# A transformer block on one core: the first folded weight is stored and loaded at earlier steps, and half of the sums of the second MLP weight stand beside the first MLP product

## The chip, the core and the metric

The kernel runs on one core of one Trainium2 chip. The core has TensorE (PE; its weight loads are PEld), VectorE (DVE), ScalarE (ACT), GpSimd (POOL) and SyncE (SP), which here only issues transfers. Each engine works through its own list of instructions in the order in which they were written, and waits at an instruction until what it needs is there. The metric is the device time of one execution in microseconds (us).

## The reference

The block computes two pre-norm sublayers in fp32 on x of 2048 x 1024:

```python
h = x + _A_ref(_layernorm(x), A_wqkv, A_w_phi, A_wo)
h2 = h + _B_ref(_layernorm(h), B_w1, B_w2)
# _A_ref: q, k, v = split(x @ wqkv), 32 heads of 32
#   pq, pk = q @ w_phi, k @ w_phi (by head)
#   phi = concat(softmax(p), softmax(-p))         # 64 features by head
#   o = phi_q (phi_k^T v) / (phi_q sum(phi_k) + 1e-6);  return o @ wo
# _B_ref: relu(x @ w1) @ w2, with w1 1024 x 3584 and w2 3584 x 1024
```

## The kernel before, in words

**Products.** Every large product is made with three matmuls of 128 x 512 (lines 181 to 183, `mm3`): each operand is cut into a high and a low half, and high x high, high x low and low x high are added up in PSUM. A weight tile of 128 x 512 that is cut so is called a unit. ACT makes the high half (L124), and POOL or DVE the low half, weight minus high half (L128). `Units` loads raw tiles into a ring of 6 and cut units into a ring of 10; a unit's place comes free when its last product is done. In an MLP stage one unit serves four products.

**Order.** All work is a list of items for TensorE: first 32 items for k and v of the first eight row tiles (four slabs of 256 columns, `kv`, eight tiles each), 16 for q (two slabs), then the same 48 for the other eight row tiles (the second half), 32 for the output projection, and then the two MLP products. In the list each item of these first stages has eight steps, a step being the three matmuls of one unit; an MLP item has four. The program counts steps from 0; step 64 opens the second kv slab, 256 the first q slab, 384, 448, 512 and 576 the kv slabs of the second half, 640 its first q slab. Everything else is hung on a step with `when(step, function)`: it is written into its engine's list behind that step's matmuls. The steps are set by hand, and they say the place in each engine's list, not a time.

**Fold.** w_phi is multiplied into the q and k weights on the chip, two blocks of 128 rows at a time (`fold_part`, p = 0 to 7). TensorE multiplies, DVE turns the result (L309, `fold_turn`) into `wp`, `fold_store` stores it to DRAM in two halves of 512 KB (wpk, L317), and `fold_ready` allows the units of that slab to be loaded (L330 and L331). The fold p = 1 belongs to the second kv slab.

**Sums of the MLP weights.** The two MLP products are made by a scheme of Strassen's kind with seven products in place of eight; it needs sums of the blocks of w1 and w2. 56 sets make them: `t_load` loads 512 KB (tile b, L357), `t_sum` makes four subtractions of 128 x 256 on POOL (L367), `t_store` stores 512 KB (t, L370). The first 28 sets belong to w1, the others to w2, whose sums are first read in the second MLP product.

**Beside the slabs.** For each kv item DVE makes the two softmaxes (tiles kmx, ke, ksm, kphi) and POOL adds phi_k up (zacc, L457). At the end of a slab of the second half DVE combines the kv state (kd, L480), which TensorE transposes (L487), and TensorE sums zacc over the rows (`z_sum`, L495). Six early units of the attention (u = 0 to 5) multiply exp(q) by that sum on POOL while later slabs run (`early_load`, `early_sums` L560, `early_reduce`, `at_den`, `early_scale` L570). `ln_power` (L229 to L231) makes 1/sqrt(var + eps) on POOL for row tiles whose statistics are taken ahead.

Of the kernel before, what the change touches and what calls it, by code (L numbers as in the profile page):

```python
# [9 lines left out]
F32 = mybir.dt.float32  # L10
# [5 lines left out]
P = 128  # L16
S = 2048
D = 1024
# [3 lines left out]
NT = S // P  # L22
HT = NT // 2
NK = D // P
NC = DFF // P
NP = NC // 2
# [113 lines left out]
def kernel(  # L140
# [17 lines left out]
    lnp = ctx.enter_context(tc.tile_pool(name="lnp", bufs=2))  # L158
# [29 lines left out]
    def do(n, k, f, *args):  # L188
        at[n, k].append((f, args))
# [17 lines left out]
    xin, xst, xnt = {}, {}, {}  # L207
# [52 lines left out]
    tsp = kps.enter_context(tc.tile_pool(name="tsum", bufs=1, side="right"))  # L260
    folds = ExitStack()
    fp = folds.enter_context(tc.tile_pool(name="fold", bufs=2))
# [89 lines left out]

    def t_load(w, p, j, place):
        cols = slice(256 * j, 256 * (j + 1))
        b = place.tile([P, 4, 256], F32, name="b", bufs=2)
        src = (w1 if w == 1 else w2)[2 * p:2 * p + 2, :, :, cols]
        sp.dma_start(b, src.rearrange("a b p f -> p (a b) f"))  # L357
        for r in range(2):
            for c in range(2):
                tsum[j, r, c] = b[:, 2 * c + r if w == 1 else 2 * r + c, :]  # L360
        tsum[j] = b
# [483 lines left out]
    def item(gen, *args, keys):  # L845
        items.append((gen, args + (keys,)))
        steps.extend((k,) for k in keys)
        return len(items) - 1

    kv_n, q_n, wo_n, up_n, down_n = {}, {}, {}, {}, {}  # L850
# [9 lines left out]
    for b, tiles in enumerate(groups):  # L860
        for hf in range(2):

            pairs = b == 0 and hf == 0
            for j in range(0, 4, 2 if pairs else 1):
# [3 lines left out]
                for half in range(2):  # L868
                    n = item(wo_pair, tiles[j:j + 2], hf, half, keys=[("wo", hf, 4 * half + k // 2) for k in range(8)])
# [18 lines left out]
    def x_part(t):  # L888
        return [x[t * P:(t + 1) * P, :]]
# [6 lines left out]
    def when(step, f, *args):  # L896

        if step < 8 * first_up:
            do(step // 8, step % 8, f, *args)
        else:  # L900
            do(first_up + (step - 8 * first_up) // 4, step % 4, f, *args)
# [4 lines left out]
    for t in range(1, NT):  # L906
        n = t - 1 if t < HT else q_n[1, t - HT] + 1
        turn = 8 * n + 1
        if t < HT:
            stages = X_STEPS.get(t, (turn - 22, turn - 12, turn - 9, turn - 6, turn, turn + 3))  # L910
        else:

            early = 80 + 16 * (t - HT)
            when(early, ln_load, ("s", t), x_part(t))
            when(early + 14, ln_stats, ("s", t))
            when(early + 14, xin.pop, ("s", t))
            when(early + 17, ln_power, ("s", t))
            load_ = turn - 88 + 8 * (t - HT) if t < HT + 4 else turn - 36
            stages = (load_, None, None, turn - 8, turn, turn + 3)
        for step, f, *args in zip(stages, (ln_load, ln_stats, ln_power, ln_norm), [("x", t)] * 4):  # L920
            if step is not None:
                when(step, f, *args, *([x_part(t)] if f is ln_load else []))
        do(n, 0, x_open, t)
        for j in range(2):
            when(stages[4 + j], ln_turn, ("x", t), j, lambda t=t: xT[t])
# [7 lines left out]
    for p, n in zip(range(1, 8), (3, 8, 12, 16, 20, 24, 28)):  # L933
        do(n, 6 if p > 1 else 7, fold_part, p)
        if p > 1:
            when(8 * n + 10, fold_turn, p, (0, 1))
        for j in range(2):
            when(8 * n + 6 + 14 + 2 * j, fold_store, p, j)
            when(8 * n + 6 + 24 + 2 * j, fold_ready, p, j)
        do(max(n - 2, 1), 0, wt_load, p, sp)  # L940


# [73 lines left out]
    for u in range(32):  # L1016
        start = 8 * (a0 + u) if u >= 8 else 8 * (last_kv + 4) + 19 * u // 2
        slack = 6 if u < 5 else 0
        for step, f in ((-8 if u < 12 else -1, at_load), (6, at_sums), (10, at_reduce), (13, at_den), (16, at_inverse), (19, at_scale),
                        (25, at_turn), (30 + slack, at_num), (32 + slack, at_low)):  # L1020
            if u >= EARLY or f in (at_load, at_scale, at_turn, at_num, at_low):
                when(max(start + step, 8 * (last_kv + 4)), f, u)
        if u < EARLY:
            start = 8 * (kv_n[1, u // 2, NT - 1] + 4 + 4 * (u % 2))
            for step, f in ((0, early_load), (9, early_sums), (14, early_reduce), (16, at_den), (18, at_inverse),
                            (20, early_scale)):
                when(start + step, f, u)
# [12 lines left out]
    up0 = 8 * first_up  # L1040
# [9 lines left out]
    def up_step(b, p, m):  # L1050

        return up0 + 4 * (up_n[b, p, m] + 1 - first_up)

    for j, m in enumerate(UP):

        for g in range(2):
            step = up0 + (8 * j + (-62, -32)[g] if j < 4 else 6 * (j - 4) + 10 + 2 * g)
# [4 lines left out]
            step = up_step(0, NP - 1, m) + 3 * j  # L1062
# [10 lines left out]

    for n, (w, p, j) in enumerate((w, p, j) for w in (1, 2) for p in range(NP) for j in range(2)):
        step = 24 + 10 * n
        if step > 8 * q_n[1, 0] - 20:
            step += 64
        far = step + 20 < 8 * q_n[0, 0]  # L1080
        when(step, t_load, w, p, j, fp if far and n % 4 > 1 else tsp)
        for k in range(4):
            when(step + (12 if far else 7) + k, t_sum, j, k)
        when(step + (19 if far else 13), t_store, w, p, j)

    for b in range(2):
        for m in DOWN:
            n = down_n[b, m, NP - 1] + 1
            name, more = {1: "x1", 5: "x4", 6: "x2", 4: "x3"}.get(m), \
# [123 lines left out]
```

## Time and profile before

| what | value |
|---|---|
| median of 3 runs | 1909.78 us (1909.72 to 1910.68) |
| the profiled execution's own time | 1910.06 us |
| its span | 1908.3 us |
| busy share PE, DVE, ACT, POOL | 99%, 55%, 39%, 51% |
| HBM traffic over the span | 225 GB/s |

A row of a timeline gives the start in us from the span's start, the duration in us, the engine, the line, the operation, the tiles (out<-in) and, in brackets, how long the engine stood idle before it and what ended that. "SPq" is the issue of a transfer by SP, not the transfer itself. A row of the waits view gives the total in us, the number of times and the longest. A row of windows gives the stretch in us, its length, then the busy us (and instructions) of PE, PEld, DVE, ACT and POOL, the granted TensorE clock, the mean share of the 16 DMA engines and GB/s.

### The profile page before, as it was taken

Reading aid. Unit: us, or ns where it says so; the run is one execution under the profiler, and the core shown is the slowest. Engines: PE = TensorE matmul, PEld = TensorE weight load, DVE = VectorE, ACT = ScalarE, POOL = GpSimd, SP = SyncE. Lnnn points to the kernel's source line nnn. Section 1 sums busy time; section 2 is a strip of 40 time slices with the busy share of each in tenths; the row PEclk is TensorE's granted clock in tenths of the full one; section 3 lists DMA queues with packets and bytes.
Section 4 is the critical chain, followed back from the end, with each engine's and each line's share of the span. In section 5 each row is a group of like instructions: output and inputs, shape, how many; then the busy total and the mean of one; then the engine's idle time right before and its main releaser. Section 6 shows DMA issues by size and latency. Waiting matters only on the chain.

```text
span 1908.3 us, 31967 instructions
## 1 busy us (share of the span) xinstructions
PE 1889.7 (99%) x11640; PEld 1539.3 (81%) x11640; DVE 1048.7 (55%) x1752; ACT 741.6 (39%) x1318; POOL 969.1 (51%) x935
## 2 busy tenths in 40 slices
PE   8999999999999999999999999999999999999999
PEld 7677788877777777888888888888888888888887
DVE  6788678767679766445544564344433333343333
ACT  4322235222223222245455564444444444444442
POOL 3688842789945988323333222222244444444443
PEclk9999999999999999999999999999999999999999
DMA  6699885656565667696776897566677677777775
GB/s 195 204 322 318 270 266 195 205 194 210 190 217 174 203 222 235 212 292 218 259 252 229 276 289 224 176 193 194 213 239 228 192 238 234 241 213 220 216 215 177
DMA packets 292733, 432.17 MB, mean 226 GB/s; under 512 B 24160, under 2 KB 150368, under 8 KB 292576
## 3 DMA queue, kind: packets, MB, share of 16 engines
q1 hardware_dynamic: 275680, 413.36, 68.8%
q10 hardware_dynamic: 16896, 16.78, 2.6%
q8 instruction: 91, 1.49, 0.3%
q14 instruction: 66, 0.54, 0.1%
HBM read 292.68 MB, written 137.36 MB: 225 GB/s over the span
## 4 chain that ended last, share of the span: by engine, by line
PE 86%; POOL 6%; DMA 4%; issue 1%; DVE 1%; ACT 1%; SPq 0%; POOLq 0%; DVEq 0%; ACTq 0%
PE mm L181 22%; PE mm L182 21%; PE mm L183 21%; PE ac L181 4%; PE ac L182 4%; PE ac L183 4%; POOL b L367 3%; PE tp L182 2%; PE tp L181 2%; PE tp L183 2%; POOL w L128 2%; DMA b<-in_w_dram 2%; PE tp L631 1%; DMA t<-b 1%; PE tp L244 1%
## 5 line engine op out<-in xcount | busy, mean ns | idle before, releaser
L128 POOL TENSOR_TENSOR w<-raw,w 128x512 fp32r<-128x512 f32 x355 | 473.6, 1336 | 730.0 <-ACT w L124 686.1
L124 ACT ACTIVATE w<-raw 128x512 fp32r<-128x512 f32 x686 | 409.4, 626 | 522.4 <-PE mm L183 249.9
L128 DVE TENSOR_TENSOR w<-raw,w 128x512 fp32r<-128x512 f32 x331 | 271.3, 820 | 533.5 <-ACT w L124 533.2
L182 PE MATMUL mm<-w,xT 128*128 128x512 f32 x768 | 302.6, 394 | 7.1 <-POOL w L128 6.8
L181 PE MATMUL mm<-w,xT 128*128 128x512 f32 x768 | 309.4, 403 | 0.0
L183 PE MATMUL mm<-w,xT 128*128 128x512 f32 x768 | 301.1, 392 | 0.0
L181 PE MATMUL mm<-hT,w 128*128 128x512 f32 x672 | 262.9, 391 | 0.0
L183 PE MATMUL mm<-hT,w 128*128 128x512 f32 x672 | 261.9, 390 | 0.0
L182 PE MATMUL mm<-hT,w 128*128 128x512 f32 x672 | 261.8, 390 | 0.0
L367 POOL TENSOR_TENSOR b<-b 128x256 f32<-128x256 f32 x224 | 184.2, 822 | 73.0 <-DMA b<-in_w_dram 63.2
L182 PEld LDWEIGHTS mm<-w,xT 128*128 128x128 f32 x768 | 145.1, 189 | 40.4 <-POOL w L128 10.7
L181 PEld LDWEIGHTS mm<-w,xT 128*128 128x128 f32 x768 | 145.1, 189 | 34.5 <-issue 3.8
L183 PEld LDWEIGHTS mm<-w,xT 128*128 128x128 f32 x768 | 145.1, 189 | 30.9 <-DVE xT L178 0.4
L181 PE MATMUL mm<-w 128*128 128x512 f32 x392 | 152.7, 390 | 0.0
L182 PE MATMUL mm<-w 128*128 128x512 f32 x392 | 152.7, 389 | 0.0
L183 PE MATMUL mm<-w 128*128 128x512 f32 x392 | 152.7, 389 | 0.0
L183 PEld LDWEIGHTS mm<-hT,w 128*128 128x128 f32 x672 | 126.2, 188 | 26.4
L181 PEld LDWEIGHTS mm<-hT,w 128*128 128x128 f32 x672 | 126.3, 188 | 25.7
L182 PEld LDWEIGHTS mm<-hT,w 128*128 128x128 f32 x672 | 126.3, 188 | 25.6
L181 PEld LDWEIGHTS mm<-w 128*128 128x128 f32 x392 | 73.6, 188 | 15.2
L183 PEld LDWEIGHTS mm<-w 128*128 128x128 f32 x392 | 73.6, 188 | 15.2
L182 PEld LDWEIGHTS mm<-w 128*128 128x128 f32 x392 | 73.6, 188 | 15.2
(165 smaller groups left out, 3111.1 us busy)
## 6 DMA issues: line engine op xcount, KB each, us to landing
raw<-t SPq DMA_DIRECT2D x224, 256.0 KB, 4.0
raw<-ad SPq DMA_DIRECT2D x196, 256.0 KB, 3.0
raw<-in_w_dram SPq DMA_DIRECT2D x168, 256.0 KB, 3.1
b<-in_w_dram SPq DMA_DIRECT2D x56, 512.0 KB, 4.9
t<-b SPq DMA_DIRECT2D x56, 512.0 KB, 4.6
ad<-c SPq DMA_DIRECT2D x112, 256.0 KB, 3.6
ad<-s SPq DMA_DIRECT2D x84, 256.0 KB, 3.9
ed<-qe ACTq DMA_DIRECT2D x32, 512.0 KB, 4.3
```

Of the source, the lines that this page charges most:

```text
L124: nc.scalar.activation(w[:, 0, :], raw[1], AF.Copy)
L128: eng.tensor_tensor(out=w[:, 1, :], in0=raw[1], in1=w[:, 0, :].bitcast(F32), op=ALU.subtract)
L181: pe.matmul(ps, a_hi, b_hi, start=first, stop=False, skip_group_check=more)
L182: pe.matmul(ps, a_hi, b_lo, start=False, stop=False, skip_group_check=more)
L183: pe.matmul(ps, a_lo, b_hi, start=False, stop=last, skip_group_check=more)
L244: pe.transpose(pt[:, k, :], xn[:, (4 * j + k) * P:(4 * j + k + 1) * P], ident)
L367: pool.tensor_tensor(out=tsum[j, *out], in0=tsum[j, *a], in1=tsum[j, *b], op=ALU.subtract)
L631: pe.matmul(banks[g][32 * c:32 * (c + 1), 0:P], kvL[rows, 4 * q + 2 * sd + h // 4, 32 * (h % 4):32 * (h % 4 + 1)], phT[rows, :, c, sd, :], ...
```

## The change

It has four parts. The store of the fold p = 1 and the release of its units are hung on earlier steps: store at 39 and 41 (before 44 and 46), release at 46 and 48 (before 54 and 56). The sets of sums get a table of steps: the first 22 stay, four stand at 264 to 294 (before, six at 244 to 294), two at 364 and 374; 14 stand at steps 10, 24 and 38 of each kv slab of the second half, with one more at step 2 of the second and third (before, 28 sets ten steps apart from 368 to 638); the last 14, all of w2, are hung on steps of the first MLP product of the second row half, 25 apart, and use the buffers `xin` of the layer norms. The early units start 4 steps (even u) or 18 steps (odd u) earlier. `ln_power` of the statistics taken ahead stands two steps later.

```diff
     def t_load(w, p, j, place):
         cols = slice(256 * j, 256 * (j + 1))
-        b = place.tile([P, 4, 256], F32, name="b", bufs=2)
+        if place is lnp:
+            b = lnp.tile([P, D], F32, name="xin").rearrange("p (a f) -> p a f", a=4)
+        else:
+            b = place.tile([P, 4, 256], F32, name="b", bufs=2)
...
-            when(early + 17, ln_power, ("s", t))
+            when(early + 19, ln_power, ("s", t))
...
         for j in range(2):
-            when(8 * n + 6 + 14 + 2 * j, fold_store, p, j)
-            when(8 * n + 6 + 24 + 2 * j, fold_ready, p, j)
+            lag = 8 * n + 6 + 2 * j + (3 if p == 1 else 0)
+            when(lag + (6 if p == 1 else 14), fold_store, p, j)
+            when(lag + (13 if p == 1 else 24), fold_ready, p, j)
...
         if u < EARLY:
-            start = 8 * (kv_n[1, u // 2, NT - 1] + 4 + 4 * (u % 2))
+            start = 8 * (kv_n[1, u // 2, NT - 1] + 3) + 4 + 18 * (u % 2)
...
-    for n, (w, p, j) in enumerate((w, p, j) for w in (1, 2) for p in range(NP) for j in range(2)):
-        step = 24 + 10 * n
-        if step > 8 * q_n[1, 0] - 20:
-            step += 64
-        far = step + 20 < 8 * q_n[0, 0]
-        when(step, t_load, w, p, j, fp if far and n % 4 > 1 else tsp)
+    sets = [(w, p, j) for w in (1, 2) for p in range(NP) for j in range(2)]
+    places = [24 + 10 * n for n in range(22)] + [264, 274, 284, 294, 364, 374]
+    slabs = [8 * kv_n[1, q, HT] for q in range(4)]
+    places += sorted([slab + step for slab in slabs for step in (10, 24, 38)] + [slabs[1] + 2, slabs[2] + 2])
+    places += [up0 + 440 + 25 * n for n in range(14)]
+    for n, (step, (w, p, j)) in enumerate(zip(places, sets, strict=True)):
+        far = n < 22
+        when(step, t_load, w, p, j, lnp if step > up0 else fp if far and n % 4 > 1 else tsp)
         for k in range(4):
             when(step + (12 if far else 7) + k, t_sum, j, k)
         when(step + (19 if far else 13), t_store, w, p, j)
```

The changed kernel's lines are numbered 3 higher from `t_load` on: L360 is the load of a set, L370 its subtraction, L373 its store.

SP, in the first slab, before (t_0 is the stored sum of the first set, wpk_75 the folded weight of the second slab, raw its units):

```order
L214 DMA xin<-in_x_dram 128x1024
L357 DMA b<-in_w_dram 128x4x256
L370 DMA t_0_310<-b 512x1x256
L317 DMA wpk_75<-wp 128x4x256
L357 DMA b<-in_w_dram 128x4x256
L317 DMA wpk_75<-wp 128x4x256
L274 DMA wt<-in_wqkT_dram 128x1024 x2
L370 DMA t_0_310<-b 512x1x256
L357 DMA b<-in_w_dram 128x4x256
L330 DMA raw<-wpk_75 128x256
L331 DMA raw<-in_wv_dram 128x256
```

The same place now:

```order
L214 DMA xin<-in_x_dram 128x1024
L360 DMA b<-in_w_dram 128x4x256
L317 DMA wpk_75<-wp 128x4x256 x2
L373 DMA t_0_310<-b 512x1x256
L360 DMA b<-in_w_dram 128x4x256
L330 DMA raw<-wpk_75 128x256
L331 DMA raw<-in_wv_dram 128x256
```

Both stores of the folded weight moved ahead of the first sum's store, and the units' loads ahead of the two loads wt, of another sum's store and of one load of a set. POOL's and ACT's lists are the same there.

POOL, at the start of the second half's first q slab, before (w is a low half, b a sum, xl the product of an early unit, smq its scale):

```order
L367 TENSOR_TENSOR b<-b 128x256 x3
L128 TENSOR_TENSOR w<-raw,w 128x512 x2
L457 TENSOR_TENSOR zacc_359<-zacc_359,kphi 128x512
L128 TENSOR_TENSOR w<-raw,w 128x512
L367 TENSOR_TENSOR b<-b 128x256
L128 TENSOR_TENSOR w<-raw,w 128x512
L367 TENSOR_TENSOR b<-b 128x256
L128 TENSOR_TENSOR w<-raw,w 128x512
L367 TENSOR_TENSOR b<-b 128x256
L128 TENSOR_TENSOR w<-raw,w 128x512
L367 TENSOR_TENSOR b<-b 128x256
L560 TENSOR_TENSOR xl<-xl,zb 128x1024
```

Now:

```order
L563 TENSOR_TENSOR xl<-xl,zb 128x1024
L370 TENSOR_TENSOR b<-b 128x256 x2
L460 TENSOR_TENSOR zacc_359<-zacc_359,kphi 128x512
L594 TENSOR_TENSOR xtz<-xtz,smq 128x32
L598 TENSOR_TENSOR qden<-xtz 128x16
L128 TENSOR_TENSOR w<-raw,w 128x512 x2
L460 TENSOR_TENSOR zacc_359<-zacc_359,kphi 128x512
L573 TENSOR_TENSOR smq<-smq,qden 128x4x8
L128 TENSOR_TENSOR w<-raw,w 128x512 x4
```

The sums between the low halves are gone, and the early unit's product and its two small products stand ahead of them. Low halves that DVE makes are not in this list; in a q slab of the second half POOL makes all.

POOL, where the moved sums begin, beside the first MLP product (the sums are written to xin):

```order
L128 TENSOR_TENSOR w<-raw,w 128x512 x17
L370 TENSOR_TENSOR xin<-xin 128x256 x4
L128 TENSOR_TENSOR w<-raw,w 128x512 x3
L370 TENSOR_TENSOR xin<-xin 128x256 x4
L128 TENSOR_TENSOR w<-raw,w 128x512 x3
```

There was nothing but low halves here; now four sums follow every three low halves, or stand singly between them, 14 times.

## The prediction

> **What bounds the kernel now.** I read the page's busy times first, then the waits of TensorE, then its timeline at each wait, then the stretches by window.
>
> ```profile
> span 1908.3 us, 31967 instructions
> PE 1889.7 (99%) x11640; PEld 1539.3 (81%) x11640; DVE 1048.7 (55%) x1752; ACT 741.6 (39%) x1318; POOL 969.1 (51%) x935
> PE mm L182 <- POOL w L128: 6.8, 6, 3.1
> PE tp L487 <- DVE kd L480: 1.4, 1, 1.4
> ```
>
> TensorE is busy 99% of the span. An edit that moves work between POOL, DVE and SP and leaves the matmuls as they are can win only what TensorE waits, and what it loses at a lower clock after a wait. The waits view names two causes within reach: a low half that POOL makes (L128), and the combined kv state of a slab that DVE makes late (L480). The timeline shows where:
>
> ```profile
> 72.53 0.50 PE L182 MATMUL mm<-w,xT 128*128 128x512 f32 x1 [0.34 <-POOL w L128]
> 74.91 0.50 PE L182 MATMUL mm<-w,xT 128*128 128x512 f32 x1 [0.73 <-POOL w L128]
> 79.65 0.80 PE L182 MATMUL mm<-w,xT 128*128 128x512 f32 x1 [3.08 <-POOL w L128]
> ...
> 422.03 0.50 PE L182 MATMUL mm<-w,xT 128*128 128x512 f32 x1 [0.50 <-POOL w L128]
> ...
> 435.15 0.92 PE L487 MATMUL tp<-ident,kd 128*128 128x128 f32 x4 [1.36 <-DVE kd L480]
> ...
> 522.29 0.50 PE L182 MATMUL mm<-w,xT 128*128 128x512 f32 x1 [1.40 <-POOL w L128]
> ```
>
> The same view of waits, for the stretch from 200 to 260 us, gives one more (at 232 us, the first q slab); the windows give the clock behind two of them, and the pace of an undisturbed stretch:
>
> ```profile
> PE mm L182 <- POOL w L128: 0.7, 1, 0.7
> ...
> 79.30:82.70 3.40, 3.05 (x7) 2.05 (x8) 3.31 (x6) 0.00 (x0) 3.40 (x4) 0.50 0.22 74
> 523.00:526.40 3.40, 3.40 (x10) 2.67 (x9) 1.12 (x1) 0.00 (x0) 3.40 (x2) 0.51 0.87 250
> 1137.00:1375.00 238.00, 238.00 (x1052) 197.19 (x1051) 101.45 (x139) 104.96 (x179) 58.18 (x44) 1.00 0.64 197
> ```
>
> The granted clock is 0.50 and 0.51 for 3.40 us behind the waits at 79 and 522 us, which costs 3.40 x 0.50 = 1.70 and 3.40 x 0.49 = 1.67 us. So the change can reach: A, second kv slab, 0.34 + 0.73 + 3.08 + 1.70 = 5.85; B, first q slab, 0.7; C, 422 us, 0.5; D, 435 us, 1.36; E, first q slab of the second half, 1.40 + 1.67 = 3.07. Together 11.5 us. From 1137 to 1375 us TensorE starts 1052 matmuls in 238 us, 0.226 us each: a step of three is 0.68 us.
>
> [...]
>
> **The first fold (term A).** SP held the store of the folded weight back:
>
> ```profile
> 46.23 1.40 DVE L309 STREAM_TRANSPOSE wp<-tp 128x256 f32<-128x256 f32 x4
> ...
> 55.34 0.60 SPq L370 DMA_DIRECT2D t<-b  x1
> 55.99 0.62 SPq L317 DMA_DIRECT2D wpk<-wp  x1
> 56.65 1.04 SPq L357 DMA_DIRECT2D b<-in_w_dram  x1
> 57.74 1.32 SPq L317 DMA_DIRECT2D wpk<-wp  x1
> 62.90 0.59 SPq L330 DMA_DIRECT2D raw<-wpk  x1
> ...
> 63.53 0.58 ACT L177 ACTIVATE xT<-tp 128x512 fp32r<-128x512 f32 x1
> 70.49 1.38 ACT L124 ACTIVATE w<-raw 128x512 fp32r<-128x512 f32 x2 [6.38 <-DMA raw<-in_wv_dram]
> ...
> 71.20 1.28 POOL L128 TENSOR_TENSOR w<-raw,w 128x512 fp32r<-128x512 f32 x1 [8.25 <-ACT w L124]
> 78.34 1.25 POOL L128 TENSOR_TENSOR w<-raw,w 128x512 fp32r<-128x512 f32 x1
> 80.70 1.72 POOL L128 TENSOR_TENSOR w<-raw,w 128x512 fp32r<-128x512 f32 x1
> ...
> 46.00:56.00 10.00, 9.64 (x93) 7.54 (x92) 9.72 (x25) 3.88 (x6) 4.81 (x9) 1.00 0.23 64
> 62.00:68.00 6.00, 6.00 (x30) 4.97 (x29) 3.73 (x8) 1.12 (x2) 0.95 (x1) 1.00 1.06 390
> ```
>
> DVE has the folded weight ready at 47.6 us, but the stores stand behind the store of a sum (55.34), which waits for POOL; they go out at 55.99 and 57.74, and the slab's first unit is asked for at 62.90. The DMA engines are used 23% from 46 to 56 us and are full from 62 to 68. In the new order both stores stand ahead of that sum's store, so they leave at about 47.7, into the idle stretch; the units follow the sum's store and one load, at 55.34 + 0.60 + 1.04 = 57.0: 5.9 us sooner. Two loads of q/k weights (wt) now stand behind four units; issued at about 62, and landed by 70.5 even at the 7 us that the unit of 63.5 took, they serve a fold at 83 us (77 in the new time).
>
> POOL's own order there does not change: from 71.20 it runs without a gap to 82.4, with sums and additions of zacc between the low halves. Moved by 5.9 it ends unit 4 at 73.7 and unit 6 at 76.5. TensorE wants unit 0's low half at 72.53 - 0.34 = 72.19, so unit 4's at 74.9 and unit 6's at 76.3. That leaves 0.2 us; ACT could begin no earlier than 64.1 (63.53 + 0.58), so the chain can move at most 6.4. Bounds: nothing left, or, if the units' transfers take back half of the lead, unit 4 late by 1.7 and unit 6 by another 1.4, with a half clock 4.8 us. I take 0.5 left: A gives 5.3.
>
> **The sums (terms B to E).** 28 of the 56 sets of sums stood in the second half of the kv and q slabs (steps 368 to 638). Now 16 stand there, 14 run beside the first MLP product, and the first half has two fewer, at steps 244 and 254. A set is a load of 512 KB, four subtractions on POOL and a store of 512 KB.
>
> ```profile
> L367 POOL TENSOR_TENSOR b<-b 128x256 f32<-128x256 f32 x95 | 78.1, 822 | 13.5 <-DMA b<-in_w_dram 9.8
> L570 POOL TENSOR_TENSOR smq<-smq,qden 128x32 f32<-128x32 f32 x6 | 2.4, 398 | 0.0
> L128 POOL TENSOR_TENSOR w<-raw,w 128x512 fp32r<-128x512 f32 x21 | 30.6, 1463 | 3.0 <-ACT w L124 3.0
> 350.00:540.00 190.00, 186.62 (x1272) 148.85 (x1271) 129.81 (x254) 50.73 (x94) 165.44 (x170) 0.99 0.63 198
> 510.46 2.56 POOL L128 TENSOR_TENSOR w<-raw,w 128x512 fp32r<-128x512 f32 x2 [1.18 <-ACT w L124]
> 512.96 1.31 POOL L457 TENSOR_TENSOR zacc<-zacc,kphi 128x512 f32<-128x512 f32 x1
> ...
> 520.98 1.26 POOL L128 TENSOR_TENSOR w<-raw,w 128x512 fp32r<-128x512 f32 x1
> ```
>
> From 350 to 550 us POOL makes 95 such subtractions, 822 ns each, and is busy 165 of 190 us. By the table of steps 12 sets (48) stay there: 47 x 0.822 = 39 us fewer, 126 of about 185. It no longer runs behind, which is what C and D are: DVE's late kd waits behind instructions that wait for POOL. Both go (1.86), D perhaps not wholly: I keep 0.2.
>
> For E the new order is two low halves, an addition, one small product, four low halves, without a sum. Beginning at 510.46 as now: 2.56 + 1.31 + 0.40 + 4 x 1.28 = 9.4, so the last ends at 519.9 and not at 522.24; TensorE wants it at 522.29 - 1.40 - 0.5 (the wait ahead of it) = 520.4. With 1.46 us for each of the four, the mean from 350 to 550 us, the last ends at 520.6, 0.2 late. I keep 0.4 of 3.07; its bounds are 0 and 1.4, the wait without the half clock. For B three sums of 0.8 us leave the queue ahead of the late unit: 0.7 comes back.
>
> The six early units keep their instructions and move 4 or 18 steps ahead, into POOL time that the sums left; eight ln_power move two steps, so that POOL waits less for DVE's statistics. No price.
>
> **What comes due elsewhere.** TensorE is 5 us earlier in a stretch where the transfers are nearly full:
>
> ```profile
> 74.00:80.00 6.00, 2.19 (x8) 1.40 (x8) 4.85 (x7) 3.08 (x6) 6.00 (x6) 0.94 0.24 72
> 100.00:150.00 50.00, 50.00 (x452) 39.71 (x451) 43.49 (x91) 13.16 (x26) 40.71 (x49) 1.00 0.95 316
> ...
> L367 POOL TENSOR_TENSOR b<-b x224: 722/739/1266, 51.8 to 531.1; 128x256 f32<-128x256 f32 x112
> 1200.82 1.30 POOL L128 TENSOR_TENSOR w<-raw,w 128x512 fp32r<-128x512 f32 x1 [4.15 <-ACT w L124]
> SPq L370 <- POOL b L367: 70.9, 30, 6.0
> ```
>
> The slabs at 128 and 177 us could then wait for sums whose loads are late: between 0 and the whole 5.3; I take 0.8, since the transfers that were bunched from 56 to 74 us are spread out. In the MLP stretch POOL makes one low half in 5.4 us and idles 4.15 ahead of each; four sums cost 2.9 to 5.1. The ring holds ten units, and one serves four steps (2.7 us), so work there runs up to 24 us ahead, four times the longest time (6.0) that SP's store of a sum has waited for POOL. 14 sets move 14.7 MB in 238 us, 62 GB/s on top of 197, below the 316 that the first slabs carry without a wait. Cost zero; if that cover were gone, a set would cost what it holds SP beyond 24 us.
>
> **The sum:** 5.3 + 0.7 + 0.5 + 1.2 + 2.7 - 0.8 = 9.6 us. The profiled execution took 1910.06 (span 1908.3 and 1.8 around it); the median shown is 0.28 lower. 1909.8 - 9.6 = 1900.2.
>
> **Rivals.** (1) The first boundary gives back half: POOL's unbroken chain stays late because the units' transfers share the engines with the wt loads. For it: 1.06 of the DMA share at 62 us; against: the 1 MB of the two stores has left that bunch. 9.6 - 4.3 = 5.3 won, 1904.5. (2) The early slabs take back the 5 us, since the loads, at 0.95 share, set the pace there: 9.6 - 4.5, 1904.7. Against: the share is 0.24 from 74 to 80 us, so there is room to load ahead just behind the first boundary. (3) The second half does not do what it says: an early unit's product now stands just ahead of a slab's low halves and waits for DVE, so C, D and E stay: 9.6 - 4.4 = 5.2, 1904.6. (4) Slower: a store of a sum on SP waits for POOL, the MLP units' loads queue behind it, and each set holds them longer than the 24 us lead. From 25 us a set costs 1 us or more, 14 sets 14: 1910 - 9.6 + 14 = 1914. Longest such wait now: 6.0.
>
> **Chances.** Forecast 0.62; rivals 1, 2 and 3 0.12, 0.11 and 0.06; slower 0.03; two of 1 to 3 together, 0.06, leave about 1 us, within 0.2%. 0.2% (3.8 us) is what a measurement of this kernel can tell from no change; each of 1 to 3 alone still wins 5 us. Faster 0.91, same 0.06, slower 0.03. Range: low end all 11.5 and a little for the restarts behind each wait, 1897; high end rivals 1 to 3, 1905.2.
>
> **What would show it.** Right: no wait at the second slab's start beyond 0.5 us; no stretch at half clock; the fold's stores near 48 us; POOL under 70% from 350 to 540 us; TensorE without a wait in the MLP stretch. Wrong: waits of L182 on POOL at about 122, 171 or 510 us, or any wait of TensorE behind the added sums.

## The result, and the profile after

The changed kernel takes 1896.35 us in the median of four executions (1895.95 to 1896.98), the kernel before, run beside it, 1910.23 (1909.72 to 1911.06): ratio 0.9927, 95% interval 0.9910 to 0.9944, 13.9 us less. In one of the sets below, run later, it took 1899.43 against 1911.4, ratio 0.9935 (0.9921 to 0.9949), 12.0 less. One of the 26 executions of the kernel before beside the first set of experiments took 3148 us at a clock of 0.556; the ratios leave it out, and it moves that set's median (1910.56) by 0.1 us. Forecast were 9.6 us less and 1897.0 at the low end of the range: direction and mechanism were right, the gain was put too small.

The page of the changed kernel, its busy times, and the whole list of TensorE's waits (total us, times, longest):

```profile
span 1894.2 us, 31951 instructions
PE 1884.1 (99%) x11640; PEld 1536.4 (81%) x11640; DVE 1064.2 (56%) x1752; ACT 741.5 (39%) x1318; POOL 979.6 (52%) x935
PE tp L244 <- ACT xn L237: 2.6, 2, 1.5
PE tp L1126 <- POOL ones L1122: 1.6, 1, 1.6
PE tp L634 <- issue: 1.1, 2, 0.8
PE tp L244 <- DVE wp L309: 0.4, 1, 0.4
PE tp L244 <- ACT xn L1142: 0.2, 1, 0.2
PE ac L278 <- DMA wt<-in_wqkT_dram: 0.2, 1, 0.2
PE mm L182 <- POOL sc L229: 0.2, 1, 0.2
```

Two lines are gone: L182 on POOL's low half (6.8 us, six times) and the transposes on DVE's kd (1.4). What is left was there before, but for 0.2 us at the program's start (8 us), for a load of q/k weights (wt).

The timeline of SP and POOL at the second kv slab, and the windows of the changed kernel that answer to those of before:

```profile
47.37 0.92 SPq L317 DMA_DIRECT2D wpk<-wp  x2
55.04 0.60 SPq L373 DMA_DIRECT2D t<-b  x1
56.40 1.00 SPq L330 DMA_DIRECT2D raw<-wpk  x1
...
72.05 1.28 POOL L128 TENSOR_TENSOR w<-raw,w 128x512 fp32r<-128x512 f32 x1
...
74.45 1.29 POOL L128 TENSOR_TENSOR w<-raw,w 128x512 fp32r<-128x512 f32 x1
...
71.50:78.70 7.20, 7.20 (x90) 5.17 (x89) 4.71 (x9) 2.17 (x4) 7.12 (x7) 1.00 0.49 124
504.80:516.60 11.80, 11.80 (x82) 9.46 (x82) 7.03 (x15) 3.12 (x5) 10.13 (x8) 1.00 0.49 153
350.00:540.00 190.00, 190.00 (x1257) 153.18 (x1256) 133.26 (x261) 52.61 (x95) 127.85 (x123) 1.00 0.48 152
1123.00:1361.00 238.00, 238.00 (x1052) 197.07 (x1051) 109.82 (x135) 103.62 (x179) 109.44 (x99) 1.00 0.76 252
```

The fold's stores leave together at 47.37, the first unit is asked for at 56.40 (before 62.90), and POOL's low half of unit 6 ends at 75.74, 0.11 us before TensorE wants it at 75.85. TensorE is busy throughout each window, at the full clock. POOL is busy 127.85 of 190 us.

Where the time went is read from the starts of the first matmuls of an item (eight steps; an item without a wait takes the same time in both kernels). Excess over the shortest of the six profiles, in us, the half clock included; the four other kernels are those of the first set of experiments:

| place (us in the kernel before) | before | after | fold alone | all but the fold | sums alone | early units alone |
|---|---|---|---|---|---|---|
| first item, 13 | 0 | 0 | 1.6 | 1.6 | 0 | 0 |
| A, 72 to 85 | 6.5 | 0 | 0.5 | 8.0 | 9.0 | 8.3 |
| B, 227 | 1.0 | 0 | 1.0 | 0 | 0 | 1.0 |
| second q slab, 272 | 0.1 | 0 | 1.2 | 0 | 0 | 0 |
| C, 417 | 0.8 | 0 | 0.8 | 0 | 0 | 1.5 |
| D, 430 | 1.8 | 0 | 1.3 | 0 | 0 | 0 |
| slab at 467 | 0 | 0 | 0 | 0 | 0 | 0.9 |
| E, 515 to 531 | 3.7 | 0 | 2.1 | 0 | 0 | 3.7 |
| second MLP product, 1393 | 0 | 0 | 0 | 0.4 | 1.2 | 0 |

A to E add up to 13.9 us, which is the whole gain; the prediction put the same places at 11.5. Term by term, waits and half clock together: A 6.50 us where the prediction has 5.85, B 0.99 for 0.7, C 0.79 for 0.5, D 1.84 for 1.36, E 3.74 for 3.07.

### The profile page after: what moved, and what is told of

It reads as the page before. It is cut to its first block, busy times and chain, and to the rows that moved or that the text cites. A ratio compares the mean times of both kernels' runs of the same rounds, so it can differ in the third digit from the quotient of the medians.

```text
span 1894.2 us, 31951 instructions
## 1 busy us (share of the span) xinstructions
PE 1884.1 (99%) x11640; PEld 1536.4 (81%) x11640; DVE 1064.2 (56%) x1752; ACT 741.5 (39%) x1318; POOL 979.6 (52%) x935
## 4 chain that ended last, share of the span: by engine, by line
PE 98%; DVE 1%; ACT 1%; POOL 0%; DMA 0%; issue 0%; SPq 0%; DVEq 0%; POOLq 0%
PE mm L181 25%; PE mm L182 25%; PE mm L183 25%; PE ac L183 4%; PE ac L181 4%; PE ac L182 4%; PE tp L183 2%; PE tp L181 2%; PE tp L182 2%; PE tp L244 1%; PE tp L634 1%; PE ac L471 1%; PE ac L634 1%; PE tp L289 0%; PE tp L1126 0%; DMA wpk<-wp 0%
## 5 line engine op out<-in xcount | busy, mean ns | idle before, releaser
L128 POOL TENSOR_TENSOR w<-raw,w 128x512 fp32r<-128x512 f32 x355 | 479.5, 1355 | 576.7 <-ACT w L124 551.7
L128 DVE TENSOR_TENSOR w<-raw,w 128x512 fp32r<-128x512 f32 x331 | 283.7, 858 | 518.2 <-ACT w L124 515.2
L182 PE MATMUL mm<-w,xT 128*128 128x512 f32 x768 | 300.0, 391 | 0.2 <-POOL sc L229 0.2
L182 PE MATMUL mm<-hT,w 128*128 128x512 f32 x672 | 261.5, 389 | 0.0
L370 POOL TENSOR_TENSOR b<-b 128x256 f32<-128x256 f32 x168 | 133.5, 795 | 90.1 <-DMA b<-in_w_dram 82.5
L182 PEld LDWEIGHTS mm<-w,xT 128*128 128x128 f32 x768 | 144.3, 188 | 30.2 <-issue 1.0
L182 PE MATMUL mm<-w 128*128 128x512 f32 x392 | 152.5, 389 | 0.0
L182 PEld LDWEIGHTS mm<-hT,w 128*128 128x128 f32 x672 | 126.2, 188 | 25.7
L370 POOL TENSOR_TENSOR xin<-xin 128x256 f32<-128x256 f32 x56 | 49.4, 882 | 108.4 <-DMA xin<-in_w_dram 101.1
L460 POOL TENSOR_TENSOR zacc<-zacc,kphi 128x512 f32<-128x512 f32 x60 | 82.7, 1378 | 11.0 <-DVE kphi L452 11.0
L182 PEld LDWEIGHTS mm<-w 128*128 128x128 f32 x392 | 73.6, 188 | 15.3
```

What stands on the lines that cost most here:

```text
L128: eng.tensor_tensor(out=w[:, 1, :], in0=raw[1], in1=w[:, 0, :].bitcast(F32), op=ALU.subtract)
L182: pe.matmul(ps, a_hi, b_lo, start=False, stop=False, skip_group_check=more)
L370: pool.tensor_tensor(out=tsum[j, *out], in0=tsum[j, *a], in1=tsum[j, *b], op=ALU.subtract)
L460: pool.tensor_tensor(out=zacc[s], in0=zacc[s], in1=phi_of[key], op=ALU.add)
```

## The experiments

### One part at a time

The fold alone (kernel before, with these lines):

```
+            lag = 8 * n + 6 + 2 * j + (3 if p == 1 else 0)
+            when(lag + (6 if p == 1 else 14), fold_store, p, j)
+            when(lag + (13 if p == 1 else 24), fold_ready, p, j)
```

> The kernel before with one part of the change, the fold's new steps (store of p = 1 at steps 39 and 41, release at 46 and 48). Theory 1: the second slab's late start is worth what lies between the starts of its matmuls, 13.67 us before against 7.17 in the changed kernel, and nothing is given back later: 6.5 us less than before, about 1903.6, with the waits at 232, 422, 435 and 522 us still there. Theory 2: it is worth what the idle times and the half clock of the profile add up to, 5.85, or the 5.3 that the prediction kept of it: 1904.2 to 1904.8. Rival: the slabs at 128 and 177 us only hold because the sums at steps 244 and 254 went too; alone, the fold gives back 2 us or more: 1906 or longer.

Measured: 1904.64 us against 1910.56, ratio 0.9969 (0.9957 to 0.9980), 5.9 less. Two rows of the waits view of this kernel; then the window from 18 to 22 us (the granted clock is the third number from the end), of the kernel before and of this kernel:

```profile
PE mm L182 <- POOL w L128: 3.4, 6, 1.4
PE tp L487 <- DVE kd L480: 0.8, 1, 0.8
```

```profile
18.00:22.00 4.00, 2.67 (x16) 2.37 (x17) 1.98 (x4) 3.48 (x7) 2.16 (x4) 1.00 0.41 117
```

```profile
18.00:22.00 4.00, 2.48 (x11) 2.29 (x12) 1.79 (x5) 3.48 (x7) 2.33 (x4) 0.76 0.36 110
```

The item at A got back 6.0 of its 6.5 us (one wait of 0.3 is left), and no wait came from 100 to 225 us: the slabs at 128 and 177 us took nothing back. A wait of 1.4 us stays at the first q slab of the second half, this time without a half clock behind it. In its place the profile has a half clock of 1.7 us at 20 us, behind a wait of 1.5 us that all kernels up to here have there. And the second q slab (272 us) loses 1.2 us, where the kernel before loses 0.1: four low halves stand in POOL's list behind a sum that waits 3.9 us for its load, and two of them come late. So the place A behaves as theory 1 says; but something was given back, less than the rival's 2 us, and the whole time is theory 2's.

All but the fold (changed kernel with the old fold lines):

> The changed kernel with the fold's steps as before. Theory 1 (independent parts, sizes from start to start): 6.5 us more than the changed kernel, about 1902.9, with the wait at 79 us and its half clock back and no wait at 422, 435 or 522 us. Theory 2 (sizes from the idle times): 5.3 to 5.85 more, 1901.7 to 1902.2. Rival: the parts help each other (slabs ahead of their transfers); the loss is 8 or more, 1904.4 or longer.

Measured: 1905.13 us, ratio 0.9971 (0.9960 to 0.9982); 5.7 more than the changed kernel took in the later set, 8.8 more than in its own comparison. The changed kernel was not run beside this one, so the times do not choose between the theories and the rival. The places say more: A is back with 8.0 us, 1.6 come from a half clock at the first item, and B to E are gone. The parts are independent in the places where they act.

The table of sums alone:

```
+        if place is lnp:
+            b = lnp.tile([P, D], F32, name="xin").rearrange("p (a f) -> p a f", a=4)
...
+    places = [24 + 10 * n for n in range(22)] + [264, 274, 284, 294, 364, 374]
+    places += sorted([slab + step for slab in slabs for step in (10, 24, 38)] + [slabs[1] + 2, slabs[2] + 2])
+    places += [up0 + 440 + 25 * n for n in range(14)]
```

> The kernel before with only the table of the sums' steps (and the buffers of the sums beside the MLP product); the fold, the early units and the statistics' power stay. Theory 1: POOL's load of sums alone made the waits at 232, 422, 435 and 522 us: 0.99 + 0.79 + 1.84 + 3.74 = 7.4 us less than before, about 1902.8. Rival: the odd early units, which stand at the very start of a slab in the kernel before, hold POOL there too; the wait at 522 us stays or comes back in part: 3 us less gain, about 1906. Theory 3: the sums beside the MLP product cost something of their own, which shows as waits of TensorE behind 1100 us.

Measured: 1906.02 us, ratio 0.9975 (0.9965 to 0.9984), 4.5 less. B, C, D and E are gone by this part alone, so the rival on the odd early units falls. The gain is smaller than their 7.4 for two reasons: A took 9.0 us in this profile and 6.5 before, with two half clocks behind it (3.4 us; before 1.7), and a new wait stands at the second MLP product:

```profile
PE mm L182 <- POOL w L128: 0.8, 1, 0.8
```

That row is of the window from 1380 to 1400 us: theory 3 holds too, with 1.2 us from start to start.

The early units and the statistics' power alone:

```
-            when(early + 17, ln_power, ("s", t))
+            when(early + 19, ln_power, ("s", t))
...
-            start = 8 * (kv_n[1, u // 2, NT - 1] + 4 + 4 * (u % 2))
+            start = 8 * (kv_n[1, u // 2, NT - 1] + 3) + 4 + 18 * (u % 2)
```

> The kernel before with only the early units' and the statistics' new steps. Theory 1: POOL is busy 165 of 190 us there and runs behind whatever their order: within 1 us of before, 1909 to 1911, the waits at 422, 435 and 522 us all there. Rival: what made the wait at 522 us was the early unit at the slab's start; then 3.7 us less, about 1906.4.

Measured: 1914.9 us, ratio 1.0022 (1.0013 to 1.0031): 4.3 us more, which neither theory had. The waits from 400 to 540 us:

```profile
PE mm L182 <- POOL w L128: 4.6, 5, 1.4
```

Before, that stretch had two such waits, 1.9 us, and one of 1.4 for kd; now it has five, and that for kd is gone. But in the profile, the shortest of the ten executions (1911.72), the stretch is no longer than before: 6.1 us at C, 467 and E, against 6.4 at C, D and E. What this profile has more is at A, 1.8 us with a second half clock. The granted clock of the ten executions is 0.9969 in the mean, that of the kernel before beside them 0.9981; over the span that is 5.9 and 3.6 us lost, so about half of the 4.3 us is half clock behind waits. That an early unit moved ahead in a full POOL queue goes in front of somebody else is a reading of the five waits, and no profile shows where the rest was lost. The reverse, the changed kernel without this part:

> The changed kernel with the early units and the statistics' power at their steps of before. Theory 1: the sums' new places alone took the waits of the second half away (the kernel with the table of sums alone had none at 418, 430 or 516 us): within 1 us of the changed kernel, apart from a half clock. Rival: the odd early units, back at the start of a slab, meet the low halves there, where the changed kernel has 0.4 us to spare at 517 us: a wait of 1 to 3 us there.

Measured: 1897.79 us, ratio 0.9932 (0.9917 to 0.9947), beside 1896.92 for another variant of the changed kernel in the same set; no wait returned at the q slab (0.59 us to spare there, 0.39 in the changed kernel). With the sums out of the way the early units' place is worth nothing that can be measured; with the sums in place it cost 4.3 us, half of that by the clock.

### Where in the slab the sums stand

```
-    places += sorted([slab + step for slab in slabs for step in (10, 24, 38)] + [slabs[1] + 2, slabs[2] + 2])
+    places += sorted([slab + step for slab in slabs for step in (24, 38, 52)] + [slabs[1] + 10, slabs[2] + 10])
```

> The changed kernel with its 14 sets in the second half's slabs moved towards the slab's end: steps 24, 38 and 52 (now 10, 24 and 38), and 10 in the second and third slab (now 2). As many sums in the same stretch; the last of each slab, with four subtractions of 0.82 us, falls on the slab's last steps. Theory 1 (place): POOL makes sums where the next slab's low halves are due, and waits of TensorE come back at some of the slab starts (418, 467, 516 us): 2 to 8 us more than the changed kernel ran beside it (1899.4 in the last set). Rival (load alone): POOL has the time in any order, under 1 us more.

Measured: 1899.94 us, ratio 0.9944 (0.9930 to 0.9959), 2 to 3 us more than the two variants run beside it (1897.79 and 1896.92), 0.5 more than the changed kernel in the set before. The executions just overlap (1898.63 to 1902.07 against 1896.32 to 1898.79), so the times are weak evidence for the low end of theory 1; the profile shows it at one place. POOL at the first q slab of the second half, changed kernel first:

```profile
502.53 1.29 POOL L460 TENSOR_TENSOR zacc<-zacc,kphi 128x512 f32<-128x512 f32 x1
503.77 0.70 POOL L573 TENSOR_TENSOR smq<-smq,qden 128x32 f32<-128x32 f32 x1
504.44 5.05 POOL L128 TENSOR_TENSOR w<-raw,w 128x512 fp32r<-128x512 f32 x4
```

```profile
506.67 1.30 POOL L128 TENSOR_TENSOR w<-raw,w 128x512 fp32r<-128x512 f32 x1
507.93 0.74 POOL L370 TENSOR_TENSOR b<-b 128x256 f32<-128x256 f32 x1
508.62 1.29 POOL L128 TENSOR_TENSOR w<-raw,w 128x512 fp32r<-128x512 f32 x1
509.87 0.74 POOL L370 TENSOR_TENSOR b<-b 128x256 f32<-128x256 f32 x1
510.57 1.29 POOL L128 TENSOR_TENSOR w<-raw,w 128x512 fp32r<-128x512 f32 x1
511.81 1.20 POOL L370 TENSOR_TENSOR b<-b 128x256 f32<-128x256 f32 x1
512.97 1.26 POOL L128 TENSOR_TENSOR w<-raw,w 128x512 fp32r<-128x512 f32 x1
```

Four low halves in one run end 0.39 us ahead of their use; with three sums between them the last comes 1.51 us late, as in the kernel before. So E is a matter of place: POOL's load from 350 to 540 us is 128.59 us here and 127.85 in the changed kernel. C and D did not come back (0.75 us came at 457), so sums at a slab's end are not enough to make them. That they are POOL's load is not shown: D is gone with the early units alone too, with all sums in place, and with 28 sets back in the slabs (next) C returns with 4.2 us and D does not. The wait was followed by a half clock (1.7 us from 514 to 518).

All 28 sets in the second half's slabs again, seven to a slab, none in the MLP stretch:

```
-    places += sorted([slab + step for slab in slabs for step in (10, 24, 38)] + [slabs[1] + 2, slabs[2] + 2])
-    places += [up0 + 440 + 25 * n for n in range(14)]
+    places += sorted([slab + step for slab in slabs for step in (2, 9, 16, 23, 30, 37, 44)])
```

> The changed kernel with no sums beside the MLP product: the 28 sets of w2 that the change spread stand in the four kv slabs of the second half, seven to a slab, at steps 2, 9, 16, 23, 30, 37 and 44, so that the last sum of a slab is due at step 54 and none at the slab's end. Theory 1 (POOL's load): POOL is busy about as in the kernel before, 160 of 190 us, runs behind, and waits for low halves come back at 400 to 530 us: 3 to 7 us more than the changed kernel. Rival (place within a slab): with no sum at the slab's end the low halves there are in time: within 1.5 us of the changed kernel, and the move into the MLP stretch was not needed.

Measured: 1927.12 us, ratio 1.0082 (1.0068 to 1.0096), 27.7 more than the changed kernel beside it and 16 more than the kernel before, which has as many sets there. Both theories missed. POOL and TensorE at the second slab of that half:

```profile
361.61 1.28 POOL L460 TENSOR_TENSOR zacc<-zacc,kphi 128x512 f32<-128x512 f32 x1
363.32 3.48 POOL L370 TENSOR_TENSOR b<-b 128x256 f32<-128x256 f32 x4 [0.43 <-DMA b<-in_w_dram]
366.76 1.27 POOL L128 TENSOR_TENSOR w<-raw,w 128x512 fp32r<-128x512 f32 x1
367.98 1.73 POOL L460 TENSOR_TENSOR zacc<-zacc,kphi 128x512 f32<-128x512 f32 x1
369.68 2.51 POOL L128 TENSOR_TENSOR w<-raw,w 128x512 fp32r<-128x512 f32 x2
...
368.08 0.79 PE L182 MATMUL mm<-w,xT 128*128 128x512 f32 x1 [3.88 <-POOL w L128]
```

The edit did not do what it was written for. The loads of a slab's sets left 5.4 to 8.7 us apart, while seven steps are 4.8 us: the tile b has two buffers, and SP waits for a store to land before the next load (65.0 us in nineteen waits from 320 to 510 us). So the seventh set, meant for step 54, was made across the slab's end, and four sums stood ahead of the low halves. It shows the price of sums at that point (3.9 us and a half clock), and nothing on whether the load without them would be harmless.

### The sums beside the MLP product

> The changed kernel with all 28 sets of w2 beside the first MLP product, 12 steps apart (8.2 us) from its step 440 to 764, and none in the slabs of the second half. Theory 1 (the cover is half used): with 14 sets the low halves there still lead by 11 us and by 1.6 at the second MLP product; with twice the sets the lead is gone, and TensorE waits for low halves behind 1120 us, 5 to 20 us in all: 1901 to 1916. Rival: the ring of ten units covers it, as the prediction held: within 1 us of the changed kernel.

The edit is `places += [up0 + 440 + 12 * n for n in range(28)]` in place of the slabs' sets and the 14. Measured: 1945.63 us, ratio 1.0181 (1.0165 to 1.0196), 46 us more than the changed kernel beside it: theory 1 in kind, more than twice its upper end in size, and not by late low halves, which in the first MLP product still led by 3.3 us. To tell density from number:

```
-    places += [up0 + 440 + 25 * n for n in range(14)]
+    places += [up0 + 440 + 12 * n for n in range(14)]
```

> The changed kernel with its 14 sets beside the MLP product 12 steps apart in place of 25 (steps 440 to 596 of it). Theory 1 (density): a set keeps POOL 3 us with sums and 7 us waiting for their load, more than the 8.2 us between sets, so the cover shrinks from set to set; as with 28 sets, TensorE's waits begin about 80 us after the first set and run to the last: the kernel with 28 sets lost some 14 us in that stretch (1204 to 1240 us), so 8 to 15 us here, waiting for ACT's and DVE's copies (c), not for low halves. Rival (number): 14 sets fit in any order, under 2 us more than the changed kernel, and none at the second MLP product's start.

Measured: 1915.48 us, ratio 1.0025 (1.0016 to 1.0035): 18 to 19 us more than the two variants of the changed kernel beside it (1897.79 and 1896.92), theory 1 in kind and above its 15 us in size. Density decides: the same 14 sets closer together turn the gain into a loss. The waits begin at 1204 us, 75 us after the load of the first set. The waits from 1100 to 1380 us, the window of the worst 60 us (POOL is busy 31.44 of them), and one wait followed back on SP, POOL and ACT:

```profile
PE mm L181 <- DVE c L774: 6.4, 4, 2.6
PE mm L181 <- ACT c L771: 5.8, 2, 3.7
POOL xin L370 <- DMA xin<-in_w_dram: 60.9, 13, 7.7
...
1200.00:1260.00 60.00, 49.90 (x201) 39.42 (x200) 21.24 (x28) 20.79 (x36) 31.44 (x33) 0.94 0.71 236
...
1191.98 0.86 SPq L360 DMA_DIRECT2D xin<-in_w_dram  x1
1193.61 2.23 SPq L343 DMA_DIRECT2D raw<-t  x2
1204.35 0.33 SPq L343 DMA_DIRECT2D raw<-in_w_dram  x1
...
1199.89 3.18 POOL L370 TENSOR_TENSOR xin<-xin 128x256 f32<-128x256 f32 x4 [7.71 <-DMA xin<-in_w_dram]
1203.03 1.29 POOL L128 TENSOR_TENSOR w<-raw,w 128x512 fp32r<-128x512 f32 x1
...
1201.85 0.63 ACT L124 ACTIVATE w<-raw 128x512 fp32r<-128x512 f32 x1 [1.17 <-DMA raw<-t]
1207.10 0.63 ACT L124 ACTIVATE w<-raw 128x512 fp32r<-128x512 f32 x1 [0.97 <-DMA raw<-in_w_dram]
1211.52 0.63 ACT L124 ACTIVATE w<-raw 128x512 fp32r<-128x512 f32 x1 [3.26 <-DMA raw<-in_w_dram]
```

POOL's next instruction is a sum whose load left at 1191.98; it stands 7.71 us and makes no low half, so no raw place comes free, and SP issues nothing from 1195.84 to 1204.35. ACT, in its own order, waits for the raw tiles of those late loads (to 1207.10 and 1211.52) with high halves which are needed only later, DVE's low half follows ACT's, and the copies of finished products (c) queue behind them. TensorE waits 2.27 us for such a copy, to 1213.53. Its wait before that, 1.39 us to 1205.53, goes back to a load of SP's row 1193.61, ahead of the stop, which took 8.1 us to land.

The load-to-sum distance, changed alone but for 25 steps by which the sets move ahead:

```
-    places += [up0 + 440 + 25 * n for n in range(14)]
+    places += [up0 + 415 + 25 * n for n in range(14)]
...
-            when(step + (12 if far else 7) + k, t_sum, j, k)
-        when(step + (19 if far else 13), t_store, w, p, j)
+            when(step + (12 if far else 17 if step > up0 else 7) + k, t_sum, j, k)
+        when(step + (19 if far else 22 if step > up0 else 13), t_store, w, p, j)
```

> The changed kernel with the 14 sets beside the MLP product 25 steps sooner and with more room between a set's load and its sums: sums 17 steps behind the load (now 7), store 22 behind (now 13). Theory 1 (POOL waits because its list holds the sums too soon behind their load): POOL's waits on those loads fall from 101 us in all and 12.6 at the longest to under 30 in all, the cover stays near that of the kernel before (17 us or more in the first MLP product), and the wait at 1379 us, 0.9 us when the changed kernel ran beside the others, is gone; time within 1.5 us of the changed kernel, since TensorE did not wait there otherwise. Rival: SP's own queue is late, and POOL waits as long whatever the steps.

Measured: 1896.92 us, ratio 0.9929 (0.9912 to 0.9945). POOL's waits on those loads, in the changed kernel and here:

```profile
POOL xin L370 <- DMA xin<-in_w_dram: 101.1, 13, 12.6
```

```profile
POOL xin L370 <- DMA xin<-in_w_dram: 5.1, 2, 3.7
```

Theory 1 holds: the waits were the distance of seven steps (4.8 us), not SP's queue. The 25 steps alone do not do it: the last variant below has them with the old distance, and POOL waits 116.3 us on those loads. The low halves of w1 (first MLP product) lead by 17.1 us at the least (11.2 in the changed kernel, 17.1 before), those of w2 by 6.95 (1.63, and 5.98 before). With the 25 steps alone these are 10.1 and 7.0: the distance gives back the lead of w1, the earlier place that of w2. The time is that of the changed kernel within what can be measured; what is won is safety, the earlier place of it where the changed kernel waited 0.9 us in the later set.

### The changed kernel once more, and a try at the start

> The changed kernel once more, on the same chip as the others of this set. Theory 1: half clock comes by chance behind a wait of a microsecond or more, and this kernel has one such wait left (17 us): most executions within 1 us of 1896.3 with clock 1.0, some 1.7 us longer. Theory 2: the half clock follows a fixed pattern of waits: all within 1 us of 1896.3.

Measured: 1897.57 to 1899.82 us, granted clock 0.999 in all four executions. Its profile has a half clock of 1.7 us behind the wait at 17 us, and two waits that the first profile did not have, 1.2 us at the q slab of E and 0.9 at the second MLP product: places where the first profile had 0.39 and 1.63 us to spare. Both theories missed the time: no execution lies within 1 us of 1896.3. That the same wait at 17 us has a half clock behind it here and had none before speaks for theory 1; the new waits neither had, and they show that those margins are within what differs from one profiled execution to another.

```
-    X_STEPS = {1: (None, None, None, None, 4, 4), ...
-               4: (9, 21, 22, 25, 27, 28), 5: (15, 25, 26, 29, 34, 36), ...
+    X_STEPS = {1: (None, None, None, None, 7, 9), ...
+               4: (9, 21, 22, 25, 29, 31), 5: (15, 25, 26, 29, 35, 37), ...
...
+    places += [up0 + 415 + 25 * n for n in range(14)]
```

> The changed kernel with the transposes of row tiles 1, 4 and 5 a few steps later (7 and 9, 29 and 31, 35 and 37; now 4 and 4, 27 and 28, 34 and 36) and the 14 sets beside the MLP product 25 steps sooner. The waits of TensorE at 17, 38 and 46 us (1.5, 1.0 and 0.4 us, and the restart behind each) go for the most part: 1.3 + 0.8 + 0.4 = 2.5 us less than the changed kernel, about 1893.9; the sums' move is worth nothing by itself but keeps the start of the second MLP product free of waits. Rival: the copies behind the transposes are then late for the next item, and nothing or less than 1 us is won.

Measured: 1900.21 us, ratio 0.9941 (0.9928 to 0.9953), 0.8 more than the changed kernel beside it. The rival was right: the later transposes hand on late copies, and a wait of 2.1 us for such a copy (xT, ahead of the fold's products at 44 us) stands where one of 1.0 had been; the first five items took 4.2 us more than in the shortest of the profiles, half clock included. The sums' move did as expected: no wait at the second MLP product. None of these kernels beats the changed one by more than can be measured.

## Why the prediction was too small

**What bounds the kernel, and where.** Right: TensorE's waits at the five places were the whole of it.

**The step that failed: the size of the terms.** The waits were priced by the idle time in brackets. The kernel before at E, TensorE's rows around the 1.40 us that the prediction quotes:

```profile
519.42 0.39 PE L181 MATMUL mm<-w,xT 128*128 128x512 f32 x1
519.93 0.50 PE L182 MATMUL mm<-w,xT 128*128 128x512 f32 x1
520.26 0.39 PE L183 MATMUL mm<-w,xT 128*128 128x512 f32 x1
520.50 0.40 PE L181 MATMUL mm<-w,xT 128*128 128x512 f32 x1
...
522.63 0.40 PE L183 MATMUL mm<-w,xT 128*128 128x512 f32 x1
```

An unbroken stretch starts a matmul every 0.23 us but shows each as 0.39 long. The bracket counts from the shown end, so it leaves out 0.17 us, and the restart takes 0.34 to the next start in place of 0.23: from 520.50 to 522.63 the loss is 1.56 + 0.11 = 1.67 us where the bracket says 1.40. And the unit before it, late by 0.23, shows no bracket at all, yet 519.42, 519.93, 520.26 are 0.51 and 0.33 apart: another 0.38. Over A to E that is 10.5 us of waits from start to start, where the brackets give 8.1. The prediction allowed "a little for the restarts" at its low end alone, when seven waits made 2.4 us of it.

**The second half of the miss: what was withheld.** 0.5 at A, 0.2 at D, 0.4 at E and 0.8 for early slabs, 1.9 in all. None of it came in the first comparison: the margins predicted at A and E were -0.2 and 0.5 us, measured 0.11 and 0.39. Since they are that thin, some of it did come in the later profile of the changed kernel (0.5 at A, 1.2 at E).

**The half clock** was counted as 3.37 us that the change removes. In the profiled execution of before it was that; as a term it is a draw, though of about that size on average: in the three later sets the kernel before has a mean clock of 0.998, 3.6 to 4.2 us lost. The changed kernel has 1.000 in all four executions of its own comparison and 0.999 in the later four, about 1.9 of the 3.1 us by which those were longer. Thirteen profiles have the same wait of 1.5 us at 17 us, and a half clock followed in eight of them. Of the four kernels with a wait of 1.4 us at E, one followed in two (the kernel before, the sums late in the slab) and none in two (the fold alone, the early units alone).

What decides it no run shows. The length of the wait does not part the cases: it is 1.5 us at 17 us in all thirteen profiles and 1.4 at E in all four.

**Terms A to E by mechanism.** A: right, order and times of SP and POOL as worked out, 56.4 against the 57.0 forecast for the first unit and 75.7 against 76.5 for the last low half. E: right, the order of POOL without sums, and shown by putting them back. C and D: the table of sums alone removes them, as forecast. That POOL's load as such made them is argued: with 28 sets back in the slabs C returns and D does not, and D also goes with the early units alone. POOL's 127.85 us of 190 stand against the 126 of 185 forecast.

**Early units, "no price".** Right for this change, wrong as a general statement: alone they cost 4.3 us, half of it by the clock. They were free only where the sums had left.

**The MLP stretch, "cost zero".** Right in time in the first comparison (in the later set 0.9 us came at the second MLP product), wrong in its argument. The cover was taken as 24 us against the longest single hold, and rival 4 set its limit there. The holds add up instead: a set took POOL about 3 us of sums and 7 us of waiting (101.1 / 14), and the low halves of its 17 us take 4. With 8.2 us between sets that does not fit, and TensorE waits although POOL never waits longer than 7.7 us there; at 25 steps a wait of 12.6 did no harm. And it waits for copies behind ACT's high halves, not for low halves.

**Rivals.** 1 (first boundary gives half back) and 2 (early slabs take the gain): no wait there in the changed kernel, and 0.3 us at the boundary, none from 100 to 225 us and 1.2 at the second q slab with the fold alone. 3 (second half unchanged): false with the sums alone. 4: not in this change, but a loss is within reach at half the spacing, by another way: a sum that waits for its load keeps POOL from the low halves (60.9 us), while with 28 sets at that spacing SP's stores waited for POOL's sums 1.6 us at the longest.

**Open:** what decides whether a half clock follows a wait; what made C and D; why A alone cost between 6.5 and 9.0 us in four profiles whose orders are equal up to there, beyond its one or two half clocks (4.8 to 6.3 us without them).

## What to carry to other kernels

Price a wait of TensorE by the distance between the starts of the matmuls around it against the undisturbed pace, not by the idle time shown (at E 1.67 us against 1.40); a unit that was late by 0.23 us there had no bracket at all, and a half clock behind a wait is a draw to be carried as a chance (eight of thirteen profiles at 17 us). Work that is hung on a filled engine "for nothing" is free only if that engine's time including its waits fits the spacing (14 sets 8.2 us apart cost 18 to 19 us here): add the wait for the work's own load, and look at what stands behind it in each list that it can stop. A longer distance between a load and its use, at no instruction more, gave back the whole lead of the first MLP product here (17.1 us, with the old distance 10.1).

## What the runs showed that was not expected

The half clock came in pieces of 3.4 us (1.7 us lost), and fell behind waits of 1.4 to 1.5 us in some executions and not in others of the same order of instructions: behind the wait of 1.5 us at 17 us in eight of thirteen profiles. A POOL that waited 7.7 us for a load of sums stopped SP's issue for 8.5 us and, through it, ACT's copies and TensorE, while POOL itself was busy 31.44 us of 60.
